# Projections inside the attention steps as two 64-row sums in two PSUM banks, one copied by ScalarE and the other added by VectorE

## The chip, the cores and the metric

The kernel runs on one core of a Trainium2 chip. The metric is the device time of that core in microseconds (us). A change of about 0.2% is the least that a measurement of this kernel can tell from no change.

The engines are named as in the profile: PE is TensorE's matmul, PEld its weight load, ACT is ScalarE, DVE is VectorE, POOL is GpSimd and SP is SyncE, which issues most DMAs here. PSUM is the memory that PE writes its sums to; it has eight banks of 128 partitions by 512 float32, and a bank must be read out by ACT or DVE before PE may start another sum in it.

## The reference

Two multi-head attentions over the same input are mixed by a gate. The sequence has S = 2048 rows, the model D = 640 features in 32 heads of 20.

```python
def attention(x, wqkv, wo):                      # once with A's weights, once with B's
    qkv = (x @ wqkv).reshape(B, S, 3, H, Dh).transpose(2, 0, 3, 1, 4)
    q, k, v = qkv[0], qkv[1], qkv[2]             # H = 32 heads, Dh = 20
    scores = einsum("bhqd,bhkd->bhqk", q, k) * Dh ** -0.5
    p = softmax(scores)
    o = einsum("bhqk,bhkd->bhqd", p, v)
    return o.transpose(0, 2, 1, 3).reshape(B, S, D) @ wo

x = A_x
g = sigmoid((x * gate_w).sum(-1, keepdims=True))
out = g * attention(x, A_wqkv, A_wo) + (1 - g) * attention(x, B_wqkv, B_wo)
```

## The kernel before

**Tiling.** The 64 heads of both attentions are worked off in 16 groups of four. A group has four blocks of 512 queries, and each block is eight steps, so there are 512 steps (`STEPS`). A step multiplies the keys of two 128-row tiles with the 512 queries of its block for four heads, which is eight sums of scores ("e" in the code, `scores`, lines L624 to L638), and takes the exponential of each with ACT out of PSUM (L635). The probabilities of the step before are multiplied with the values in two blocks "V" of four matmuls (`values`, L645 to L651), which collect in a bank of their own, `acc`. The largest score of each row, which the exponential subtracts, is found some 15 steps ahead by up to eight more sums of scores a step ("m", `max_mm`, L558 to L587). DVE reduces those (L585); for a part of them ACT takes a relu (L578) and DVE adds a second sum to it while it reduces (L582).

**Row groups.** A score needs only 60 or 64 rows of the array, because a head has 20 features (as high and low fp16 parts, and four rows more for the maximum). So sums of scores come in pairs: one in rows 0 to 63 and one in rows 64 to 127, at the same time and in two banks. A "V" and a projection use all 128 rows.

**Projections.** Inside the steps the next groups' queries, keys and values are projected, and the output projection of finished groups is made. Each is cut into slots "X": one sum of 9 to 15 matmuls over 128 rows (five tiles of 128 features, three products of high and low fp16 parts) in one bank, which one instruction reads. There are 456 such slots in the steps: 216 of `project_chunk` (L384 to L411, 176 or 168 columns, ACT copies at L402), 112 of the 128 of `project_v` (L519 to L535, 160 columns, ACT copies at L530), and 128 of `out_tiles` (L685 to L730; 64 of 160 columns that ACT copies at L715, 64 of 320 columns that DVE adds to the earlier output at L717). All their matmuls are issued by `mms` (L368 to L377, the matmul at L375). The first projections, ahead of the steps, go through the same lines with 512 columns.

**What sets the order.** The instructions are issued in an order that is written out by hand, and each engine works its own in that order. A string per step says where e, m, V and X stand:

```python
STEP = ("e0 m1 V e1 m0 e0 m1 e1 m0 e0 m1 e1 m0 V e0 m1 e1 m0",
        "X e0 m1 m0 e1 m0 m1 V m1 e0 e1 m0 e1 e0 V m0 e1 e0 m1",
        "X m0 m1 e0 m1 e0 e1 V e1 e0 m1 m0 V e1 m0 m1 m0 e0 e1 X")
```

The digit is the row group. The first string is for a step without a projection, the second for one slot, the third for two. Which string a step takes is set by how much is due (`behind`, L1044). The banks are given out by a clock that the program runs at build time: `take` (L122) picks among seven banks the one that comes free first by that clock, `give` (L133) says when a reader will be done with it, and `tick_score` and `tick_block` (L137 and L143) advance PE's time. `tick_block` adds `T_MODE` = 0.1 us on both sides of work on 128 rows. The clock only picks banks; the order of the work doesn't hang on it.

Of the kernel before, what the change touches and what calls it, by code (L numbers as in the profile page):

```python
# [61 lines left out]
def kernel(  # L62
# [18 lines left out]
    psum = ctx.enter_context(tc.tile_pool(name="psum", bufs=1, space=PSUM))  # L81
# [18 lines left out]
    acc = psum.tile([P, QB], F32, name="acc")  # L100
# [21 lines left out]
    def take():  # L122

        i = min((k for k in range(NB) if k not in held), key=lambda k: free_at[k])
        held.add(i)
        return i, banks[i]

# [32 lines left out]
    def scales(maxima, n, then):  # L160

        for _ in range(REST):
            yield
        yield PRODUCT
        i, pt = take()
        nc.tensor.transpose(pt[:n, :P], maxima[:, :n], ident)
        tick_block(0.1, free_at[i])
        yield
        e = wts.tile([5, 8], F32, name="e", tag="scl", bufs=2)
        nc.vector.tensor_reduce(e[:n, 0:1], pt[:n, :P], axis=AX.X, op=OP.max)  # L170
        give(i, spend("dve", 0.3, clock["done"]))
        spend("dve", 1.0)
        powers(e.bitcast(I32)[:n, :], 1)
        dg = wts.tile([5, 2, 5], F32, name="dg", tag="scd", bufs=2)
        for k in range(2):
            nc.vector.tensor_scalar(dg[:n, k, :n], ident[:n, :n], e[:n, 3 + k:4 + k], None, op0=OP.mult)
        for _ in range(REST):
            yield
        yield PRODUCT
        i, pb = take()  # L180
        tick_block(0.1, free_at[i])
        for k in range(2):
            nc.tensor.matmul(pb[:, k * n:(k + 1) * n], ones[:n, :], dg[:n, k, :n], start=True, stop=True)  # L183
        yield
        both = wts.tile([P, 10], F32, name="both", tag="scb", bufs=2)
        nc.vector.tensor_copy(both[:, :2 * n], pb[:, :2 * n])
        give(i, spend("dve", 0.2, clock["done"]))
        then(both[:, :n], both[:, n:2 * n])
# [179 lines left out]
    def mms(i, out_ap, pairs, cost):  # L368

        if now[0] >= 0:  # L370
            tick_block(len(pairs) * cost * T_SCORE, free_at[i])
        for k, (a, b) in enumerate(pairs):
            if now[0] < 0:
                tick_block(cost * T_SCORE, free_at[i])
            nc.tensor.matmul(out_ap, a, b, start=(k == 0), stop=(k == len(pairs) - 1))  # L375
            if now[0] < 0:
                yield  # L377
# [6 lines left out]
    def project_chunk(w, hi, lo, ch):  # L384

        wh, wl = w
        def pairs(n):
            if now[0] < 0:
                return ([(wh[:, c, :], b[:, c, n]) for c in range(NC) for b in (xh, xl)]
                        + [(wl[:, c, :], xh[:, c, n]) for c in range(NC)])  # L390
            return [(a[:, c, :], b[:, c, n]) for c in range(NC) for a, b in ((wh, xh), (wh, xl), (wl, xh))]

        t0 = ch * QB
        if now[0] >= 0:
            f = work.tile([P, QB], F32, name="fs")
            for k in range(3):
                if k:
                    yield
                m = slice(PARTS[k], PARTS[k + 1])
                i, pt = take()  # L400
                yield from mms(i, pt[:, m], pairs(slice(t0 + m.start, t0 + m.stop)), 0.34)
                nc.scalar.activation(f[:, m], pt[:, m], AF.Copy, scale=QKS)  # L402
# [116 lines left out]
    def project_v(gg, j):  # L519

        wh, wl = blk["v", gg]
        w = 161 if gg == 0 else 160
        for u in range(2):
            if u and now[0] >= 0:
                yield
            n = slice((j + u) * P, (j + u + 1) * P)
            i, pt = take()
            yield from mms(i, pt[:, :w], [(a[:, c, n], b[:, c, :w]) for c in range(NC) for a, b in
                                          ((xh, wh), (xh, wl), (xl, wh))], 0.33)
            nc.scalar.activation(V[gg % 2][:, j + u, :, 0:DH], pt[:, :160].rearrange("p (h d) -> p h d", h=2 * GH),  # L530
                                 AF.Copy, scale=QKS)
            give(i, spend("act", 0.25, clock["done"]))
            v_done.add((gg, j + u))
            if gg == 0:
                nc.scalar.activation(gates[:, 0, j + u:j + u + 1], pt[:, 160:161], AF.Exp, scale=inv_g)  # L535
# [16 lines left out]
    relus, relu_at = {}, {}  # L552
# [5 lines left out]
    def max_mm(u, ch, heads=(0, 1)):  # L558
# [9 lines left out]
        for j in heads:  # L568
            two = u < NS or ch < 2 and (j == 0 or g == 0)
            i, pt = take()  # L570
            ready = tick_score(j, i)
            r = slice(64 * j, 64 * j + 60)
            k = KD[g % 2 if ch == 0 else 1][r, pair] if two and ch % 2 == 0 else KT[g % 2][r, pair, ch * QB:(ch + 1) * QB]
            nc.tensor.matmul(pt, QT[g % 2][r, pair, q0:q0 + P], k, start=True, stop=True)  # L574
            m = mparts[g, qb][:, pair, j, t, ch:ch + 1]
            if two and ch % 2 == 0:
                relus[u, j] = start.tile([P, QB], F32, name="rl0", bufs=4) if u < NS else work.tile([P, QB], F32, name="rl", bufs=2)
                nc.scalar.activation(relus[u, j], pt, AF.Relu)  # L578
                back = relu_at[u, j] = spend("act", T_EXP, ready)
            elif two:  # L580
                rl = relus.pop((u, j))
                nc.vector.tensor_tensor_reduce(rl, pt, rl, 1.0, LOW, OP.add, OP.max, m)  # L582
                back = spend("dve", T_MAX, max(ready, relu_at.pop((u, j))))
            else:
                nc.vector.tensor_reduce(m, pt, axis=AX.X, op=OP.max)  # L585
                back = spend("dve", T_MAX, ready)
            give(i, back)  # L587
# [36 lines left out]
    def scores(G, kk, pair, heads=(0, 1)):  # L624
# [3 lines left out]
        for j in heads:  # L628
# [3 lines left out]
            nc.tensor.matmul(et, KT[g % 2][r, pair, kt * P:(kt + 1) * P],  # L632
                             QT[g % 2][r, pair, qb * QB:(qb + 1) * QB], start=True, stop=True)
            pt = pp.tile([P, QB], F32, name="pt")
            nc.scalar.activation(pt, et, AF.Exp, scale=factor(g // 4))  # L635
# [49 lines left out]
    def out_tiles(job, t, state):  # L685
# [17 lines left out]
        def products():  # L703
            wh, wl = wo_parts[z]
            for k in range(0, D, width):
                if k:
                    yield
                n = slice(k, k + width)
                i, pt = take()
                yield from mms(i, pt[:, :width], [(o[:p, a, c - c0], w[:p, c, n])  # L710
                                                  for c in range(c0, c1) for p in (P if c < full else 48,)
                                                  for a, w in ((0, wh), (0, wl), (1, wh))], width / QB)
                f = f_o[z][:, t:t + 1]
                if first:
                    nc.scalar.activation(y[:, n], pt[:, :width], AF.Copy, scale=f)  # L715
                else:
                    nc.vector.scalar_tensor_tensor(y[:, n], pt[:, :width], f, y[:, n], op0=OP.mult, op1=OP.add)  # L717
                give(i, spend("act" if first else "dve", 0.08 + width / 900, clock["done"]))
# [51 lines left out]
    def take_last():  # L770
# [5 lines left out]
        for t in range(4):  # L776
            nc.tensor.matmul(pt[:, 4 * t:4 * t + 4], ot[:, t * P:(t + 1) * P], one, start=True, stop=True)
        rc = work.tile([P, 16], F32, name="sq", bufs=2)
        nc.vector.reciprocal(rc, pt[:, :16])
        give(i, spend("dve", 0.3))  # L780
        i, pt = take()
        nc.tensor.transpose(pt[:16, :P], rc, ident)
        rt = wts.tile([16, P], F32, name="rt", tag="rt", bufs=1)
        nc.scalar.activation(rt, pt[:16, :P], AF.Copy)
        give(i, spend("act", 0.3))
        i, pt = take()
        for t in range(4):
            nc.tensor.matmul(pt[:, t * P:(t + 1) * P], picks[0].rearrange("p k e -> p (k e)")[:, t * P:(t + 1) * P], rt,
                             start=True, stop=True)
        o = work.tile([P, 2, QB], F16, name="on", bufs=2)  # L790
        for t in range(4):
            c = slice(t * P, (t + 1) * P)
            nc.vector.tensor_tensor(ot[:, c], ot[:, c], pt[:, c], op=OP.mult)
# [8 lines left out]
    def last_tiles(qb, o):  # L802
        wh, wl = wo_parts[2]
        for t in range(4):
            c = slice(t * P, (t + 1) * P)
            f = f_o[1][:, 4 * qb + t:4 * qb + t + 1]
            for half in range(2):
# [4 lines left out]
                for k, (a, w) in enumerate(((0, wh), (0, wl), (1, wh))):  # L812
                    nc.tensor.matmul(pt[:, :320], o[:, a, c], w[:, n], start=(k == 0), stop=(k == 2))  # L813
                if half and qb == NQ - 1 and t < 3:
                    part = pp.tile([P, QB], F32, name="pt")[:, :320]
                    nc.scalar.activation(part, pt[:, :320], AF.Copy, scale=f)
                    nc.gpsimd.tensor_tensor(y, y, part, op=OP.add)
                    give(i, spend("act", 0.42, clock["done"]))
                else:
                    nc.vector.scalar_tensor_tensor(y, pt[:, :320], f, y, op0=OP.mult, op1=OP.add)  # L820
# [35 lines left out]
    def turn(j0, c):  # L856
# [3 lines left out]
        for u in range(4):  # L860
            tick_block(0.11, free_at[i])
            nc.tensor.transpose(pt[:, u * P:(u + 1) * P], xs[:, j0 + u, c * P:(c + 1) * P], ident)  # L862
# [100 lines left out]
    start_stack.close()  # L963

# [212 lines left out]
```

## Time and profile before

| | |
|---|---|
| time, median of 3 runs | 2834.94 us (2834.72 to 2834.99) |
| span of the profiled execution | 2832.8 us, some 2.1 us less than the median |
| granted clock of TensorE | 0.996 |
| busy: PE, ACT, DVE, POOL | 98%, 89%, 86%, 24% |
| chain that ended last | PE 91%, DVE 5%, ACT 1% |

A profile row has the engine, the line in the code, the operation, its output and input tiles, their shape and the count; then the busy time in us, the mean of one in ns, and the idle time before with what ended it. A row of a timeline has the start in us, the duration in us, and then the same. Instructions of one kind that overlap or follow at once are merged into one row with their count. Durations of matmuls contain their way through the array, so that the distance between two starts tells the pace, not the duration.

### The profile page before, as it was taken

How to read it: one execution, taken by the hardware profiler on the slowest of the kernel's cores; microseconds unless marked ns; L12 is line 12 of the kernel's file. 1: busy time of each engine (PE TensorE's matmuls, PEld its weight loads, DVE VectorE, ACT ScalarE, POOL GpSimd, SP SyncE). 2: the span in 40 equal slices, each digit the busy share in tenths (PEclk: the TensorE clock that was granted, in tenths of full speed). 3: DMA queues.
4: the chain of work that ended last, by engine and by line, in shares of the span. 5: the costliest groups of instructions: out<-in, count | busy, mean ns of one | idle time of the engine just before them, and what ended most of it. 6: DMA issues, size and time to landing. Idle time of an engine off the chain costs nothing.

```text
span 2832.8 us, 62443 instructions
## 1 busy us (share of the span) xinstructions
PE 2773.1 (98%) x23362; PEld 970.8 (34%) x23362; DVE 2443.8 (86%) x4763; ACT 2529.7 (89%) x5122; POOL 671.8 (24%) x914
## 2 busy tenths in 40 slices
PE   6999999999999999999999999999999999999998
PEld 3533223342323323343233333334333333332222
DVE  6688999879999898988989888887888989989982
ACT  3799999989999999989999999998899999888887
POOL 5312113231221212233431111222112233120011
PEclk9999999999999999999999999999999999999999
DMA  4110101001020101202021020211202112122222
GB/s 135 35 45 7 39 6 42 16 16 29 13 52 16 37 11 27 47 13 50 17 56 44 14 60 16 48 37 24 49 15 61 38 38 70 55 71 60 63 60 74
DMA packets 167170, 113.71 MB, mean 40 GB/s; under 512 B 102224, under 2 KB 140808, under 8 KB 166864
## 3 DMA queue, kind: packets, MB, share of 16 engines
q1 hardware_dynamic: 164320, 108.09, 15.6%
q8 instruction: 183, 3.00, 0.4%
q0 software_dynamic: 1600, 0.96, 0.2%
q14 instruction: 123, 1.01, 0.1%
q10 hardware_dynamic: 944, 0.66, 0.1%
HBM read 48.89 MB, written 26.61 MB: 27 GB/s over the span
## 4 chain that ended last, share of the span: by engine, by line
PE 91%; DVE 5%; ACT 1%; DMA 1%; POOL 1%; issue 1%; SPq 0%; POOLq 0%; DVEq 0%; ACTq 0%
PE acc L650 34%; PE bank L375 20%; PE bank L632 19%; PE bank L574 17%; DVE mpart L585 3%; ACT pt L635 1%; DVE rl L582 1%; DMA xs<-in_A_x_dram 0%; ACT rl L578 0%; DMA wv<-in_A_wqkv_dram 0%; DVE ot L736 0%; PE bank L813 0%; PE bank L183 0%; PE bank L862 0%; DVE wmax L227 0%
## 5 line engine op out<-in xcount | busy, mean ns | idle before, releaser
L635 ACT ACTIVATE pt<-bank 128x512 f32<-128x512 f32 x4096 | 2157.5, 614 | 155.0 <-PE bank L632 75.1
L585 DVE TENSOR_REDUCE mpart<-bank 128x1 f32<-128x512 f32 x2976 | 1867.8, 681 | 264.3 <-PE bank L574 167.1
L650 PE MATMUL acc<-pt,v 128*21 128x512 f32 x8192 | 1082.0, 600 | 3.4 <-DVE ot L736 3.1
L632 PE MATMUL bank<-qt,kt 64*128 64x512 f16 x4096 | 1056.3, 380 | 11.9 <-ACT pt L635 4.5
L574 PE MATMUL bank<-kt,qt 60*128 60x512 f16 x3536 | 1013.0, 380 | 4.0 <-DVE mpart L585 0.7
L574 PEld LDWEIGHTS <-qt 60*128 60x128 f16 x4096 | 235.4, 94 | 686.6 <-issue 629.0
L632 PEld LDWEIGHTS <-kt 64*128 64x128 f16 x4096 | 248.1, 94 | 456.7 <-issue 322.8
L582 DVE CUSTOM_DVE_ANT_0 rl<-bank,rl 128x512 f32<-128x512 f32 x560 | 377.5, 678 | 20.5 <-ACT rl L578 8.2
L578 ACT ACTIVATE rl<-bank 128x512 f32<-128x512 f32 x560 | 329.8, 595 | 14.6 <-PE bank L574 12.3
L744 POOL TENSOR_TENSOR ot<-ot,sq 128x512 f32<-128x512 f32 x63 | 66.0, 1047 | 993.0 <-DVE sq L741 993.0
L650 PEld LDWEIGHTS acc<-pt,v 128*21 128x21 f32 x8192 | 143.0, 99 | 434.6 <-issue 421.5
L375 PE MATMUL bank<-xx,wbh 128*128 128x168 f16 (+2 forms) x2240 | 280.1, 244 | 3.2 <-ACT xx L866 1.9
L375 PE MATMUL bank<-xx,wbl 128*128 128x168 f16 (+2 forms) x1120 | 252.8, 243 | 0.0
L375 PEld LDWEIGHTS <-wbh 128*128 128x128 f16 x2240 | 183.6, 98 | 86.8 <-issue 79.8
L574 PE MATMUL bank<-kd,qt 60*128 60x512 f16 x560 | 203.6, 381 | 1.7 <-DMA kd<-dd 1.2
L375 PE MATMUL bank<-wvh,xx 128*128 128x160 f16 (+1 forms) x1280 | 155.4, 234 | 0.5 <-ACT pt L635 0.3
L375 PE MATMUL bank<-woh,o_in 128*128 128x160 f16 (+1 forms) x960 | 155.7, 256 | 0.0
L375 PEld LDWEIGHTS <-xx 128*128 128x128 f16 x1920 | 131.6, 97 | 52.7 <-issue 49.4
L404 POOL CAST cq<-fs 128x512 f16<-128x512 f32 x60 | 36.6, 609 | 446.0 <-ACT fs L402 444.0
L375 PE MATMUL bank<-wvl,xx 128*128 128x160 f16 (+1 forms) x640 | 137.3, 231 | 0.6 <-POOL wvl L315 0.6
L375 PEld LDWEIGHTS <-o_in 128*128 128x128 f16 (+1 forms) x1440 | 104.0, 97 | 75.3 <-issue 62.2
L402 ACT ACTIVATE fs<-bank 128x168 f32<-128x168 f32 (+1 forms) x216 | 67.5, 313 | 56.6 <-PE bank L375 40.0
(131 smaller groups left out, 1305.2 us busy)
## 6 DMA issues: line engine op xcount, KB each, us to landing
y_scr<-y_out SPq DMA_DIRECT2D x32, 320.0 KB
kt<-cq SPq DMA_DIRECT2D x120, 80.0 KB
o_scr<-on SPq DMA_DIRECT2D x240, 40.0 KB
kt<-cq SPq DMA_DIRECT2D x136, 40.0 KB
xs<-in_A_x_dram SPq DMA_DIRECT2D x8, 640.0 KB
o_in<-o_scr SPq DMA_DIRECT2D x32, 160.0 KB
y_out<-y_scr SPq DMA_DIRECT2D x16, 320.0 KB
xx<-y_scr SPq DMA_DIRECT2D x16, 320.0 KB
```

The costliest lines, as they stand in the source:

```text
L375: nc.tensor.matmul(out_ap, a, b, start=(k == 0), stop=(k == len(pairs) - 1))
L402: nc.scalar.activation(f[:, m], pt[:, m], AF.Copy, scale=QKS)
L404: nc.gpsimd.tensor_copy(hi, f)
L574: nc.tensor.matmul(pt, QT[g % 2][r, pair, q0:q0 + P], k, start=True, stop=True)
L578: nc.scalar.activation(relus[u, j], pt, AF.Relu)
L582: nc.vector.tensor_tensor_reduce(rl, pt, rl, 1.0, LOW, OP.add, OP.max, m)
L585: nc.vector.tensor_reduce(m, pt, axis=AX.X, op=OP.max)
L632: nc.tensor.matmul(et, KT[g % 2][r, pair, kt * P:(kt + 1) * P], QT[g % 2][r, pair, qb * QB:(qb + 1) * QB], start=True, stop=True)
L635: nc.scalar.activation(pt, et, AF.Exp, scale=factor(g // 4))
L650: nc.tensor.matmul(acc[32 * h:32 * h + VW, :], V[(g // 2) % 2][:, kt, (g % 2) * GH + h, :], ptiles.pop((G, kk, h)), start=(kt == 0), stop= ...
L744: nc.gpsimd.tensor_tensor(t3, t3, sq.unsqueeze(2).to_broadcast([P, 16, 32]), op=OP.mult)
```

## The change

In the steps, each slot's sum over 128 rows becomes two sums: one over rows 0 to 63, the other over rows 64 to 127, issued in turn (`halves_of`). Each goes to a bank of its own. The two banks must be neighbours, and `take_two` picks the pair whose later bank comes free first. Afterwards ACT copies the first bank to the target and DVE adds the second to it (`summed_halves`); where DVE added the sum before, it now adds both banks one after the other. The seven banks are one tile of seven parts in the steps, so that an instruction's access can lie in two of them, and the kernel itself states which readers don't depend on each other (`read`, `apart`). The number of columns, of slots and the strings are as before. A slot of 15 matmuls with 15 weight loads has now 30 of each.

```diff
+    def take_two():
+        i = min((k for k in range(NB - 1) if k not in held and k + 1 not in held),
+                key=lambda k: (max(max(free_at[k:k + 2]), clock["pe"]), abs(free_at[k] - free_at[k + 1])))
+        held.update((i, i + 1))
+        return (i, i + 1), store[0][:, i:i + 2]
...
+    def halves_of(pairs, w):
+        ik, two = take_two()
+        t = max(clock["pe"], max(rows_free), max(free_at[i] for i in ik))
+        parts = [[(a[p0:min(p0 + 64, a.shape[0])], b[p0:min(p0 + 64, a.shape[0])]) for a, b in pairs if a.shape[0] > p0]
+                 for p0 in (0, 64)]
+        for k in range(len(parts[0])):
+            for j in range(2):
+                if k < len(parts[j]):
+                    matmul(two[:, j, :w], *parts[j][k], start=(k == 0), stop=(k == len(parts[j]) - 1))
+        rows_free[:] = [t + len(parts[0]) * w / QB * T_SCORE] * 2
+        clock["pe"], clock["done"] = t, rows_free[0] + T_READY - T_SCORE
+        return ik, two[:, :, :w]
+
+    def summed_halves(ik, two, w, scale, to, shape=lambda x: x):
+        read(ik[:1], nc.scalar.activation(to, shape(two[:, 0]), AF.Copy, scale=scale))
+        give(ik[0], spend("act", 0.08 + w / 900, clock["done"]))
+        read(ik[1:], nc.vector.scalar_tensor_tensor(to, shape(two[:, 1]), scale, to, op0=OP.mult, op1=OP.add),
+             keep=[recent[-1][0]])
+        give(ik[1], spend("dve", 0.08 + w / 960, clock["act"]))
...
@@ project_chunk
-                m = slice(PARTS[k], PARTS[k + 1])
-                i, pt = take()
-                yield from mms(i, pt[:, m], pairs(slice(t0 + m.start, t0 + m.stop)), 0.34)
-                nc.scalar.activation(f[:, m], pt[:, m], AF.Copy, scale=QKS)
-                give(i, spend("act", 0.25, clock["done"]))
+                w = PARTS[k + 1] - PARTS[k]
+                ik, two = halves_of(pairs(slice(t0 + PARTS[k], t0 + PARTS[k + 1])), w)
+                summed_halves(ik, two, w, QKS, f[:, PARTS[k]:PARTS[k + 1]])
...
@@ out_tiles
                 if first:
-                    nc.scalar.activation(y[:, n], pt[:, :width], AF.Copy, scale=f)
+                    summed_halves(ik, two, width, f, y[:, n])
                 else:
-                    nc.vector.scalar_tensor_tensor(y[:, n], pt[:, :width], f, y[:, n], op0=OP.mult, op1=OP.add)
-                give(i, spend("act" if first else "dve", 0.08 + width / 900, clock["done"]))
+                    done = clock["done"]
+                    for j in range(2):
+                        read(ik[j:j + 1], nc.vector.scalar_tensor_tensor(y[:, n], two[:, j], f, y[:, n], op0=OP.mult,
+                                                                         op1=OP.add))
+                        give(ik[j], spend("dve", 0.08 + width / 960, done))
...
+    psum_start.close()
+    psum = ctx.enter_context(tc.tile_pool(name="psum_steps", bufs=1, space=PSUM))
+    store.append(psum.tile([P, NB, QB], F32, name="bank"))
+    banks[:] = [store[0][:, i] for i in range(NB)]
```

Four pieces of the order show what moves. In all of them a row is an instruction with its output and inputs, and in brackets stand the engines on whose semaphores it waits. `bank_89` to `bank_95` are the seven banks of before; `bank` is the one tile of after.

PE before, at the start of a slot of a value projection, behind a V; four sums of scores stand between the V and the slot:

```order
L650 MATMUL acc<-pt,v_86 21x512 x4
L574 LDWEIGHTS qt_80
L574 MATMUL bank_91<-kt_82,qt_80 128x512 [waits DVE_49]
L632 LDWEIGHTS kt_82
L632 MATMUL bank_95<-qt_80,kt_82 128x512 [waits Activation_49]
L632 LDWEIGHTS kt_82
L632 MATMUL bank_92<-qt_80,kt_82 128x512 [waits DVE_49]
L574 LDWEIGHTS qt_80
L574 MATMUL bank_93<-kt_82,qt_80 128x512 [waits Activation_49]
L375 LDWEIGHTS xx
L375 MATMUL bank_90<-wvh,xx 128x160 [waits Activation_49]
```

The slot takes one bank, `bank_90`, which none of the four sums ahead of it used.

PE after, at the start of the same slot, from the first sum behind the V:

```order
L157 LDWEIGHTS qt_83
L157 MATMUL bank<-kt_85,qt_83 128x512 [waits DVE_49]
L157 LDWEIGHTS kt_85
L157 MATMUL bank<-qt_83,kt_85 128x512 [waits Activation_49]
L157 LDWEIGHTS kt_85
L157 MATMUL bank<-qt_83,kt_85 128x512 [waits DVE_49]
L157 LDWEIGHTS qt_83
L157 MATMUL bank<-kt_85,qt_83 128x512 [waits Activation_49]
L157 LDWEIGHTS xx
L157 MATMUL bank<-wvh,xx 128x160 [waits Activation_49]
L157 LDWEIGHTS xx
L157 MATMUL bank<-wvh,xx 128x160 [waits DVE_49]
```

The slot now waits for two banks. Its first half takes the bank of the first `qt_83,kt_85` sum of this piece, the third ahead of the slot, so that it waits for that sum's exponential; its second half takes a bank that DVE read before the V.

PE after, behind the same slot:

```order
L157 MATMUL bank<-qt_83,kt_85 128x512
L157 LDWEIGHTS qt_83
L157 MATMUL bank<-kt_85,qt_83 128x512
L157 LDWEIGHTS qt_83
L157 MATMUL bank<-kd_87,qt_83 128x512 [waits DVE_49]
L157 LDWEIGHTS kt_85
L157 MATMUL bank<-qt_83,kt_85 128x512 [waits Activation_49]
L157 LDWEIGHTS qt_83
L157 MATMUL bank<-kt_85,qt_83 128x512 [waits DVE_49]
L157 LDWEIGHTS qt_83
L157 MATMUL bank<-kt_85,qt_83 128x512 [waits Activation_49]
L721 MATMUL acc<-pt,v_89 21x512 x4
```

With two banks in the slot, the first five sums take the five others, and the sixth, the last ahead of the V, waits for ACT's copy of the slot's first bank. Before, the slot's one bank was taken again only behind the V.

DVE after, between the two slots of that value projection:

```order
L656 TENSOR_REDUCE mpart<-bank 128x1 [waits PE_49] x2
L442 SCALAR_TENSOR_TENSOR v_89<-bank,v_89 128x8x20 [waits Activation_49]
L656 TENSOR_REDUCE mpart<-bank 128x1 [waits PE_49] x4
L651 ISA rl,mpart<-bank,rl 128x512 [waits PE_49]
L651 ISA mpart 128x1
L656 TENSOR_REDUCE mpart<-bank 128x1 [waits PE_49] x2
L442 SCALAR_TENSOR_TENSOR v_89<-bank,v_89 128x8x20 [waits Activation_49]
```

The additions at L442 are new on DVE; each waits for ACT's copy, and the reductions of the maximum stand behind it.

More of the change, by code (lines that the diff above doesn't have):

```diff
@@ L126, in take, with apart, on_bank, matmul @@
         return i, banks[i]
+    def take_two():
[3 more added lines that the diff above has]
+        return (i, i + 1), store[0][:, i:i + 2]
+    store, last_read = [], {}
+    fresh, recent = set(), []
+    def apart(ins, keep):
+        for r, engine in recent:
+            if r not in keep and engine != ins.engine:
+                tc.declare_no_dep(ins, r, reason="a reader of another bank")
+    def on_bank(out, ins, alone=True):
+        if store:
+            i = out.offset // QB
+            if alone:
+                apart(ins.ins, last_read.get(i, []))
+            fresh.add(i)
+        return ins
+    def matmul(out, a, b, start=True, stop=True, alone=True):
+        return on_bank(out, nc.tensor.matmul(out, a, b, start=start, stop=stop), alone)
+    def transpose(out, a, alone=True):
+        return on_bank(out, nc.tensor.transpose(out, a, ident), alone)
+    def read(banks_read, ins, keep=(), alone=True):
+        name = ins.ins.name
+        if store:
+            for i in banks_read:
+                if i in fresh:
+                    fresh.discard(i)
+                    last_read[i] = []
+                last_read[i].append(name)
+            if alone:
+                apart(ins.ins, keep)
+            recent.append((name, ins.ins.engine))
+            del recent[:-24]
+        return name
     def spend(engine, cost, ready=0.0):
@@ L526, in project_v @@
             n = slice((j + u) * P, (j + u + 1) * P)
[L527 to L532, printed above, removed]
+            pairs = [(a[:, c, n], b[:, c, :w]) for c in range(NC) for a, b in ((xh, wh), (xh, wl), (xl, wh))]
+            to = V[gg % 2][:, j + u, :, 0:DH]
+            if now[0] >= 0:
+                ik, two = halves_of(pairs, w)
+                summed_halves(ik, two, w, QKS, to, lambda x: x.rearrange("p (h d) -> p h d", h=2 * GH))
+            else:
+                i, pt = take()
+                yield from mms(i, pt[:, :w], pairs, 0.33)
+                nc.scalar.activation(to, pt[:, :160].rearrange("p (h d) -> p h d", h=2 * GH), AF.Copy, scale=QKS)
+                give(i, spend("act", 0.25, clock["done"]))
+                if gg == 0:
+                    nc.scalar.activation(gates[:, 0, j + u:j + u + 1], pt[:, 160:161], AF.Exp, scale=inv_g)
             v_done.add((gg, j + u))
[L534 to L535 removed]
     def sigmoids():
```

68 lines of the change are left out of this document (33 added, 35 removed).

## The prediction

> **What bounds the kernel now.** I read the page's busy times and its chain first, then the waits, then the timeline of single steps, and last the busy times of two stretches.
>
> ```profile
> span 2832.8 us, 62443 instructions
> PE 2773.1 (98%) x23362; PEld 970.8 (34%) x23362; DVE 2443.8 (86%) x4763; ACT 2529.7 (89%) x5122; POOL 671.8 (24%) x914
> PE 91%; DVE 5%; ACT 1%; DMA 1%; POOL 1%; issue 1%; SPq 0%; POOLq 0%; DVEq 0%; ACTq 0%
> PE bank L632 <- ACT pt L635: 4.5, 16, 0.5
> PE bank L632 <- DVE mpart L585: 2.7, 12, 0.2
> ACT pt L635 <- PE bank L632: 75.1, 275, 1.1
> DVE mpart L585 <- PE bank L574: 167.1, 300, 8.7
> ```
>
> PE is busy for 98% of the span and is 91% of the chain. The last four rows are waits (who waits, for whom, sum in us, count, longest): PE waits for a bank in only 28 places with 7.2 us together, while ACT and DVE wait for PE far longer. So PE sets the end, with seven banks in turn, and its waits for banks are nearly nothing. A step with one projection slot shows how PE's time goes:
>
> ```profile
> 1303.68 0.39 PE L574 MATMUL bank<-kt,qt 60*128 60x512 f16 x1
> 1303.69 0.60 PE L632 MATMUL bank<-qt,kt 64*128 64x512 f16 x2
> 1303.91 0.38 PE L574 MATMUL bank<-kt,qt 60*128 60x512 f16 x1
> 1304.22 0.32 PE L375 MATMUL bank<-xx,wbh 128*128 128x168 f16 x2
> ...
> 1305.25 0.24 PE L375 MATMUL bank<-xx,wbl 128*128 128x168 f16 x1
> 1305.42 0.39 PE L632 MATMUL bank<-qt,kt 64*128 64x512 f16 x1
> 1305.42 0.39 PE L574 MATMUL bank<-kt,qt 60*128 60x512 f16 x1
> 1305.64 0.38 PE L574 MATMUL bank<-kd,qt 60*128 60x512 f16 x1
> ```
>
> Pairs of sums (one in each row group) start 0.22 us apart: 1305.42 to 1305.64. The slot's 15 matmuls start from 1304.22 to 1305.25, so 0.0725 us apart (1.03/14, rounded by the ends). The last pair ahead of the slot started at 1303.91 and would have let the next pair start at 1304.13; the slot's first matmul starts at 1304.22, 0.09 later. Its last would have been through by 1305.32, and the next pair starts at 1305.42, 0.10 later. So a slot occupies PE for 1305.42 − 1304.13 = 1.29 us, of which 0.19 are the two changes between work on half the rows and work on all.
>
> ```profile
> 1303.68:1308.90 5.22, 5.22 (x51) 1.87 (x47) 4.38 (x9) 4.92 (x11) 1.76 (x2) 1.00 0.23 51
> 1002.70:1007.56 4.86, 4.50 (x36) 1.08 (x33) 4.72 (x11) 4.50 (x11) 0.83 (x3) 1.00 0.02 4
> ```
>
> These rows are the step with that slot and one without a slot (length; busy PE, PEld, DVE, ACT, POOL; the clock, 1.00). With a slot PE is busy throughout, ACT for 4.92 of 5.22 us and DVE for 4.38. Without one PE has gaps, and ACT and DVE set the pace.
>
> **The change, part by part.** Durations are of the profiled execution, whose span of 2832.8 us lies 2.1 us under the median of 2834.94; my sum is added to the median.
>
> *The two halves on PE.* The matmuls of a slot double from 15 to 30, but two go side by side, as pairs of scores do. The trace has no 64-row sum of 168 columns. From below: the pair takes as long as one matmul, 0.0725 us. From above: the halves, with a weight load each, go one after another, 0.145 us. Scores decide for the lower end: a pair with two loads and 512 columns needs 0.22 us, and 512 columns at the slot's pace are 0.0725 × 512/168 = 0.221. I add 0.004 us per pair for the second chain, since the fixed part of a matmul may not be shared: 15 × 0.0765 = 1.15 us.
>
> One rule on this stands in the Trainium skill, "TensorE: Matmul & The Clock Gate", section "LDWEIGHTS (loading the stationary operand)": a load's time goes by its columns, about columns/1.2 ns, and not by its rows; for 128 columns that is 107 ns, so a half would load as long as a whole, and two loads in series would be 213 ns a pair. By that the slot would be an estimated 3.2 us and the kernel some 870 us slower. The trace disagrees for loads that lie under matmuls, since load and matmul together need 0.0725 us there.
>
> *The changes of rows that go.* If a slot works on half rows there is no change of mode at either end: 0.19 us per run of slots. Of 456 slots in the steps, 48 steps carry two, one at each end, which lie next to a neighbour; I count 411 runs. The gain is 411 × 0.19 = 78 us, less 456 × 15 × 0.004 = 27: −51 us. ACT's 4.92 us of a 5.22 us step are the floor of it: 5.09 still lies above.
>
> *DVE's additions.* 216 + 112 + 64 = 392 new additions of 160 to 176 columns, and 64 more of 320.
>
> ```profile
> L717 DVE SCALAR_TENSOR_TENSOR xx<-bank,f_o,xx 128x320 f32<-128x320 f32 x32 | 17.4, 547 | 25.6 <-PE bank L632 20.3 <-PE bank L375 5.0
> L867 DVE SCALAR_TENSOR_TENSOR xx<-bank,both,xx 128x512 f16<-128x512 f32 x20 | 14.5, 748 | 5.2 <-ACT xx L866 5.1
> 1304.11 1.29 DVE L585 TENSOR_REDUCE mpart<-bank 128x1 f32<-128x512 f32 x2 [0.36 <-PE bank L632]
> L585 DVE TENSOR_REDUCE mpart<-bank 128x1 f32<-128x512 f32 x2976 | 1867.8, 681 | 264.3 <-PE bank L574 167.1
> ```
>
> From 320 to 512 columns the same kind grows by 201 ns, 1.05 ns a column, so 168 columns need 547 − 152 × 1.05 = 0.39 us. Two reductions of 681 ns take 1.29 us together, so some 0.07 of an instruction overlap with the next: 0.32 us. In sum 392 × 0.32 + 64 × 0.47 = 155 us on DVE. It is hidden where the slots are: there DVE goes from 4.38 to 4.70 of 5.09 us. The cover is DVE's idle 0.84 us in such a step; without it the 155 would stand on the path. Each addition waits for ACT's copy, and the reductions queue behind it; the copy starts right behind the slot (next fence), so this too falls into DVE's idle time. I take +10 us for steps where DVE is behind anyway, with bounds of 0 and 155.
>
> *The sixth sum behind the slot.* ACT's copies stay 392 in number and in width, but now one is waited for. In the order of after, the five sums behind a slot take the five free banks, and the sixth takes the bank that ACT copies. This is so in 311 of the 392 copied slots; in the others a V lies between.
>
> ```profile
> 1302.39 3.04 ACT L635 ACTIVATE pt<-bank 128x512 f32<-128x512 f32 x6 [0.20 <-PE bank L632]
> 1305.52 0.31 ACT L402 ACTIVATE fs<-bank 128x168 f32<-128x168 f32 x1
> 1305.84 0.60 ACT L635 ACTIVATE pt<-bank 128x512 f32<-128x512 f32 x1
> 1000.21 0.60 ACT L635 ACTIVATE pt<-bank 128x512 f32<-128x512 f32 x1 [0.33 <-PE bank L574]
> 1000.86 0.37 PE L632 MATMUL bank<-qt,kt 64*128 64x512 f16 x1 [0.25 <-ACT pt L635]
> ```
>
> The copy ends at 1305.83, 0.51 us behind the slot's stream (1305.32). The last two rows give the time from a reader's end to PE's start, 1000.81 to 1000.86: 0.05. So that bank is back at 0.56, and the sixth sum, in the third pair, is due at 0.44: +0.12 × 311 = +37 us. Slots that DVE alone reads are longer in DVE (0.55 twice); 41 of them have a sum that comes that early, up to 0.36 late, of which I take two thirds: +10 us.
>
> *Banks that are too young at the slot's start.* This is the largest term. A slot needs two neighbouring banks at once. Before, it took the bank free longest, seldom used by the last six sums. In the order of after, 145 of 455 slots take a pair of which one bank belongs to one of the last six sums, with neither a V nor a slot between: 1, 10, 35, 54, 36 and 9 of them for one to six sums back. A bank is held for at least 0.38 (the sum), 0.03 (1305.42 + 0.39 to 1305.84, the exponential's start), 0.61 (the exponential; page mean below) and 0.05 (release): 1.07, say 1.08 us. A sum k back started 0.11k earlier, so the slot, and PE in order behind it, waits 1.08 − 0.11k: 0.97 + 10 × 0.86 + 35 × 0.75 + 54 × 0.64 + 36 × 0.53 + 9 × 0.42 = 93 us.
>
> ```profile
> L635 ACT ACTIVATE pt<-bank 128x512 f32<-128x512 f32 x4096 | 2157.5, 614 | 155.0 <-PE bank L632 75.1
> L632 PE MATMUL bank<-qt,kt 64*128 64x512 f16 x4096 | 1056.3, 380 | 11.9 <-ACT pt L635 4.5
> ```
>
> From below this is 0, if the time comes back in steps that ACT bounds anyway; from above, a hold of 1.5 us, when the reader has another exponential ahead of it (0.506 us each, 3.04/6), gives 162 us. I stay at 93, because in a step with a slot PE has no gap in which to make up for it. What is late next is ACT: it runs dry while PE waits.
>
> *The rest.* One PSUM tile with its own statements on dependences moves no instruction; PE's order shows waits for the readers of the very bank alone. I cost it at nothing: no engine but PE would have to cover a wrong wait, and it would be a wait of PE for a bank. POOL's and SP's instructions and the DMAs stay as they are.
>
> Sum: −51 + 37 + 10 + 93 + 10 = +99 us; 2834.9 + 99 = 2934 us, 3.5% slower.
>
> **The rivals.**
>
> *A. The banks come back in time: faster.* The mechanism is the slack between banks and PE: if a pair of banks is back within 0.66 us on average (six sums at 0.11), neither the slot nor the sixth sum waits. For it speaks that PE hardly waits for a bank now (7.2 us); against it that the exponential alone holds a bank 0.61 us beyond the sum's 0.38. Then −51 + 10 remain: 2794 us. It decides from where the waits of 93 + 47 fall under 41 us.
>
> *B. The waits are absorbed in part.* A step without a slot is bound by ACT, and PE's lead there may pay for a wait at the next slot's start. With a quarter to half of the 140 us of waits: −51 + 10 + 35 to 70, 2829 to 2864 us. For it: PE's 4.50 of 4.86 us in such a step. Against it: slots come in most steps (378 of 512 by the strings).
>
> *C. The halves don't go side by side at this size.* The change then doesn't do what it says. With one load and matmul after another a slot is 15 × 0.145 = 2.18 us, against 1.29: +0.89 × 456 = +406, and fewer waits for banks: about 3240 us. For it: four PE instructions each 0.0725 us are more than any row here shows in a long stretch. Against it: pairs of scores.
>
> *D. DVE becomes the bound.* The 155 us come on top of the waits, since reductions hold their banks longer: some 3080 us. For it: 4.72 of 4.86 us DVE busy in a step without a slot. Against it: no slot stands there.
>
> **How the numbers follow.** The forecast has 0.62, B 0.18, A 0.10, C 0.06, D 0.04. The time is the forecast's, 2934. Its own range is 2865 (waits at half, DVE's at 10) to 3010 (a hold of 1.5 us gives 162 in place of 93). The range takes in B down to 2835 and leaves out A, C, D: 0.20. About 0.2%, 5.7 us, is the least that a measurement can tell from no change. Faster: A and a sixth of B, 0.13; same: 0.05, out of B; slower: the rest, 0.82.
>
> **What would show it.** Right: a pace of some 0.0765 us for pairs in a slot and no gap at its ends where the banks are old; PE's waits for banks rise from 7 to over 100 us, mostly ahead of a slot's first two matmuls and of the sixth sum behind it; ACT's and DVE's waits for PE grow; DVE's busy sum is some 150 us more; the busy share of PE falls under 95%. Wrong: a pace of pairs above 0.09 us (C), waits of PE under 40 us (A), DVE busy for over 95% of steps with a slot (D), or waits of DVE's additions for ACT that hold reductions back for longer than DVE's idle time.

## The result, and the profile after

The changed kernel takes 2983.55 us (2982.59 to 2986.14), the kernel before 2834.97: 1.0526 times as long, with a 95% interval from 1.0511 to 1.0541, or 149 us more. The forecast was 2934 us.

The page of the changed kernel, its chain and its waits (who waits for whom, sum in us, count, longest):

```profile
span 2984.1 us, 75456 instructions
PE 2826.7 (95%) x29626; PEld 1055.3 (35%) x29626; DVE 2574.5 (86%) x5219; ACT 2504.9 (84%) x5122; POOL 672.9 (23%) x914
PE 71%; DVE 14%; ACT 11%; issue 2%; DMA 1%; POOL 1%; SPq 0%; DVEq 0%; ACTq 0%; POOLq 0%
PE bank L157 <- ACT pt L706: 50.4, 162, 0.8
PE bank L157 <- DVE mpart L651: 24.2, 55, 1.1
PE bank L157 <- DVE mpart L656: 23.0, 57, 0.6
ACT pt L706 <- PE bank L157: 202.7, 503, 2.0
DVE fs L442 <- ACT fs L440: 137.1, 192, 9.3
```

PE was 91% of the chain and is now 71%; nearly all of the 20 points went to DVE (5% to 14%) and ACT (1% to 11%). These are the readers of banks that PE now waits for: 7 us of such waits before, 98 us in the three rows here. L157 is the one line from which the matmuls of sums and slots are now issued. Two slots in one place show both halves of the story:

```profile
1306.50 0.61 PE L721 MATMUL acc<-pt,v 128*21 128x512 f32 x4
1307.05 0.39 PE L157 MATMUL bank<-qt,kt 64*128 64x512 f16 x1
1307.05 0.60 PE L157 MATMUL bank<-kt,qt 60*128 60x512 f16 x3
1307.49 0.38 PE L157 MATMUL bank<-qt,kt 64*128 64x512 f16 x2
1308.36 0.32 PE L157 MATMUL bank<-xx,wbh 64*128 64x168 f16 x4 [0.49 <-DVE mpart L651]
...
1309.45 0.33 PE L157 MATMUL bank<-xx,wbh 64*128 64x176 f16 x4
...
1310.51 0.26 PE L157 MATMUL bank<-xx,wbl 64*128 64x176 f16 x2
1310.59 0.38 PE L157 MATMUL bank<-kd,qt 60*128 60x512 f16 x1
1310.60 0.38 PE L157 MATMUL bank<-kt,qt 60*128 60x512 f16 x1
```

The gain is there. The first slot's 15 pairs start at 1308.36 and the second slot's at 1309.45: 1.09 us or 0.0727 a pair (0.0725 within the rounding of the rows), and the pair of scores behind the second slot starts at 1310.59, one pair's time (0.075 for 176 columns) behind its last. No time is lost to a change of rows at either end. The loss stands ahead of the first slot. Its rows were free at 1307.49 + 0.22 = 1307.71, but it starts at 1308.36, since one of its two banks had been written by a sum of the burst at 1307.05 and was still being read by DVE:

```profile
1306.16 1.29 DVE L656 TENSOR_REDUCE mpart<-bank 128x1 f32<-128x512 f32 x2 [0.42 <-PE bank L157]
1307.61 0.69 DVE L651 CUSTOM_DVE_ANT_0 rl<-bank,rl 128x512 f32<-128x512 f32 x1 [0.16 <-PE bank L157]
1307.47 1.57 ACT L706 ACTIVATE pt<-bank 128x512 f32<-128x512 f32 x3 [0.36 <-PE bank L157]
```

DVE is done with that bank at 1308.30, and PE starts 0.06 later. The profile's 0.49 is the time in which PE did nothing at all; the slot is 0.65 late, because the last sums were still running for a part of it. Where only one half has to wait, less than half of it shows as idle:

```profile
1294.20 0.38 PE L157 MATMUL bank<-qt,kt 64*128 64x512 f16 x2
1294.42 0.23 PE L157 MATMUL bank<-xx,wbh 64*128 64x168 f16 x1
1294.82 0.30 PE L157 MATMUL bank<-xx,wbh 64*128 64x168 f16 x3 [0.18 <-ACT pt L706]
```

The first half starts its first matmul at 1294.42, and everything behind stands until 1294.82: 0.40 late, 0.18 of it idle. So I counted lateness instead, for every sum and slot in the steps: its start less the time at which its rows were free (the start of what ran there before, plus the columns of that at the pace of 0.0692 us for 160 and 0.0725 for 168). In the kernel before, the change of rows ahead of a slot (0.09 us in the timeline of the prediction) is not counted as lateness.

| late, in us, over the whole kernel | before | after |
|---|---|---|
| ahead of slots | 3.5 | 162 |
| of these, in slots with a bank from the last six sums, with neither V nor slot between | 1.5 (4 slots) | 109 (146 slots) |
| fourth to sixth sum behind a slot | 30 | 100 |

158 + 70 us more lateness, less the 78 us that the prediction counts for the two changes of rows, is 150 us; the spans differ by 151.3. That the two agree so closely is in part chance. The order of the program has 402 runs of slots, not 411, and 389 of them have a change ahead and 400 one behind, which makes some 75 us at 0.09 and 0.10. The twelfth sum behind a slot, the last ahead of the second V, is later by another 10 us than before and not in the table, and lateness of the two row groups at the same time is added up.

### The profile page after: what moved, and what is told of

Read it like the earlier page. It is cut to its first block, busy times and chain, and to the rows that moved or that the text cites. A ratio compares the mean times of both kernels' runs of the same rounds, so it can differ in the third digit from the quotient of the medians.

```text
span 2984.1 us, 75456 instructions
## 1 busy us (share of the span) xinstructions
PE 2826.7 (95%) x29626; PEld 1055.3 (35%) x29626; DVE 2574.5 (86%) x5219; ACT 2504.9 (84%) x5122; POOL 672.9 (23%) x914
## 3 DMA queue, kind: packets, MB, share of 16 engines
q14 instruction: 127, 1.04, 0.1%
## 4 chain that ended last, share of the span: by engine, by line
PE 71%; DVE 14%; ACT 11%; issue 2%; DMA 1%; POOL 1%; SPq 0%; DVEq 0%; ACTq 0%; POOLq 0%
PE bank L157 46%; PE acc L721 25%; ACT pt L706 10%; DVE mpart L656 9%; DVE rl L651 2%; ACT rl L647 1%; DVE ot L808 1%; DMA xs<-in_A_x_dram 0%; DVE ob L819 0%; DVE y_out L788 0%; DVE xx L788 0%; DMA wv<-in_A_wqkv_dram 0%; DVE wmax L276 0%; PE bank L160 0%; ACT fs L440 0%
## 5 line engine op out<-in xcount | busy, mean ns | idle before, releaser
L157 PE MATMUL bank<-qt,kt 64*128 64x512 f16 x4096 | 1089.4, 379 | 14.3 <-ACT pt L706 4.2
L157 PE MATMUL bank<-kt,qt 60*128 60x512 f16 x3536 | 1060.6, 378 | 7.5 <-DVE mpart L656 1.1
L157 PEld LDWEIGHTS <-qt 60*128 60x128 f16 x4096 | 260.7, 94 | 688.9 <-issue 656.5
L157 PEld LDWEIGHTS <-kt 64*128 64x128 f16 x4096 | 269.0, 94 | 416.1 <-issue 326.7
L157 PE MATMUL bank<-xx,wbh 64*128 64x168 f16 (+2 forms) x4400 | 294.5, 238 | 45.6 <-ACT pt L706 16.0
L157 PEld LDWEIGHTS <-wbh 64*128 64x128 f16 (+1 forms) x4400 | 230.8, 94 | 116.1 <-issue 86.9
L157 PE MATMUL bank<-xx,wbl 64*128 64x168 f16 (+2 forms) x2200 | 258.2, 237 | 0.0
L157 PE MATMUL bank<-kd,qt 60*128 60x512 f16 x560 | 202.8, 380 | 1.9 <-DMA kd<-dd 1.2
L157 PE MATMUL bank<-wvh,xx 64*128 64x160 f16 (+1 forms) x2400 | 165.4, 230 | 27.6 <-ACT pt L706 14.7
L442 DVE SCALAR_TENSOR_TENSOR fs<-bank,fs 128x168 f32<-128x168 f32 (+1 forms) x216 | 72.3, 335 | 138.2 <-ACT fs L440 137.1
L157 PE MATMUL bank<-woh,o_in 64*128 64x160 f16 (+2 forms) x1856 | 159.5, 250 | 23.9 <-ACT pt L706 14.6
L157 PEld LDWEIGHTS <-xx 64*128 64x128 f16 (+1 forms) x3600 | 146.4, 94 | 72.1 <-issue 55.5
L157 PEld LDWEIGHTS <-o_in 64*128 64x128 f16 (+1 forms) x2784 | 123.9, 94 | 81.0 <-issue 56.4
```

Of the source, the lines that this page charges most:

```text
L157: return on_bank(out, nc.tensor.matmul(out, a, b, start=start, stop=stop), alone)
L442: read(ik[1:], nc.vector.scalar_tensor_tensor(to, shape(two[:, 1]), scale, to, op0=OP.mult, op1=OP.add), keep=[recent[-1][0]])
```

## The experiments

The theory: the halves gain what they should, and the banks take it back, because two of seven are wanted at once, and neighbours at that. Rival 1: VectorE's additions cost it. Rival 2: the one PSUM tile with its stated dependences makes false waits. Times are medians, with the ratio to the kernel before on the same chip and its 95% interval.

### Any two banks

```diff
     def take_two():
-        i = min((k for k in range(NB - 1) if k not in held and k + 1 not in held),
-                key=lambda k: (max(max(free_at[k:k + 2]), clock["pe"]), abs(free_at[k] - free_at[k + 1])))
-        held.update((i, i + 1))
-        return (i, i + 1), store[0][:, i:i + 2]
+        ik = tuple(sorted((k for k in range(NB) if k not in held), key=lambda k: free_at[k])[:2])
+        held.update(ik)
+        return ik, [banks[i] for i in ik]
```

> The slots keep their two halves, ScalarE's copy and VectorE's addition, but the two banks need not be neighbours: each slot takes the two banks that come free first. Theory (waits for banks that are too young, because neighbours are wanted): the 162 us that PE lost ahead of the slots in the changed kernel fall to 30 to 70 us, the sixth sum behind the slot still waits (some 50 us), so 2850 to 2890 us. Rival 1 (VectorE's additions are what costs): they stay, so over 2950 us. Rival 2 (the one PSUM tile and its stated dependences make false waits): they stay, 2984 us.

2893.12 us, 1.0207 (1.019 to 1.0224): 90 us of the 149 come from the demand for neighbours alone. Page and waits of this kernel:

```profile
PE 2806.2 (97%) x29626; PEld 1058.4 (37%) x29626; DVE 2569.2 (89%) x5219; ACT 2496.9 (86%) x5122; POOL 671.7 (23%) x914
PE bank L156 <- ACT pt L705: 20.6, 105, 0.5
PE bank L156 <- DVE mpart L655: 6.8, 26, 0.5
```

The lateness ahead of slots falls from 162 to 52 us, as expected; the additions are all still there. Rival 2's 2984 and rival 1's 2950 are both ruled out as the main cause. But 2893 lies just above the range, and the fourth to sixth sum behind a slot are now 123 us late, not 100: a part of the wait that went ahead of the slot comes back behind it.

### Whole slots in the one tile

In short, at each of the projections:

```diff
-    ik, two = halves_of(pairs, w)
-    summed_halves(ik, two, w, scale, to)
+    i, pt = take()
+    for k, (a, b) in enumerate(pairs):
+        matmul(pt[:, :w], a, b, start=(k == 0), stop=(k == len(pairs) - 1))
+    read([i], nc.scalar.activation(to, shape(pt), AF.Copy, scale=scale))
```

> The slots are whole again (one sum over 128 rows in one bank, one reader), but the seven banks are one tile with the stated dependences, as in the changed kernel. Theory: 2835 us, within 6 us. Rival 2 (false waits from the one tile): more than 2850 us, up to 2984 us if it were all of the loss. Rival 1 says nothing here but 2835 us, since there are no additions.

2834.57 us, 1.0004 (0.9994 to 1.0013). The tile and its statements cost nothing with whole slots. With halves, the run with any two banks has the same tile and the same statements and is 90 us faster, so rival 2 is out as the main cause.

### The additions alone, and the changed kernel nearly without them

Whole slots with an addition of 0 times the same bank behind the copy:

```diff
     read([i], nc.scalar.activation(to, shape(pt), AF.Copy, scale=scale))
+    read([i], nc.vector.scalar_tensor_tensor(to, shape(pt), 0.0, to, op0=OP.mult, op1=OP.add), keep=[recent[-1][0]])
```

> The slots are whole, as in the run with one tile, and behind ScalarE's copy VectorE adds the same bank times 0 to the target: the additions alone, 392 of them, with their wait for the copy, but one bank only. Theory (the additions are hidden in VectorE's idle time): VectorE's busy sum rises by some 130 us, the time by 0 to 25 us, 2835 to 2860 us. Rival 1 (the additions cost): 2930 to 2985 us.

2866.03 us, 1.0114 (1.0097 to 1.013), 32 us more; DVE's busy time rises from 2444.0 us (whole slots in the one tile) to 2530.7. A little over the theory's range, far under rival 1's. The other way round, the changed kernel with an addition of one column, which leaves the rest of the second half's sum out of the result:

```diff
-    read(ik[1:], nc.vector.scalar_tensor_tensor(to, shape(two[:, 1]), scale, to, op0=OP.mult, op1=OP.add),
+    a = shape(two[:, 1])
+    one = (slice(None),) + (slice(0, 1),) * (len(a.shape) - 1)
+    read(ik[1:], nc.vector.scalar_tensor_tensor(to[one], a[one], scale, to[one], op0=OP.mult, op1=OP.add),
```

> The changed kernel, neighbours and all, but the addition takes one column alone, so that the second half's sum is left out of the result but for that column. Theory: VectorE's busy sum falls by some 60 to 110 us, and as its second bank comes back earlier only by some 0.2 us behind the slot, the time falls by 0 to 25 us: 2955 to 2984 us. Rival 1: the time falls by most of what VectorE gains, to under 2910 us.

2973.64 us, 1.0493 (1.0476 to 1.0511): 10 us less. The same cut in the kernel with any two banks:

> Any two banks, but the addition takes one column alone, so that the second half is left out of the result but for that column. Theory: the additions cost in this kernel about what they cost alone (32 us), less the wait for the copy that stays: 2865 to 2885 us. If the additions make up the most of what is left (58 us over the kernel before and the 78 us of gain), under 2850 us; if they are hidden, 2890 us.

2884.56 us, 1.0173 (1.0156 to 1.019): 9 us less than with any two banks, where I had expected 8 to 28. So the width of the additions is worth some 10 us in both kernels. Most of these 10 us show at one place: the twelfth sum behind a slot, 10 us later than before in the changed kernel, is only 3 us later with the narrow addition. That the additions cost 32 us alone points to what a narrow addition keeps, the wait for the copy and a bank that comes back later, though no run shows the two apart. In the run with the additions alone the sixth sum behind a slot is 34 us late in place of 18, the twelfth is 7 us later than before and the fifth 3 us, together 26 of the 32; the rest was not traced. Rival 1 is out as the main cause: the additions' share is 10 us by their width, and 32 with all that they bring in whole slots. No run has the halves without any addition.

### A second bank kept out of use

```diff
     i, pt = take()
+    held_too[i] = take()[0]
...
     give(i, spend("act", 0.25, clock["done"]))
+    give(held_too[i], free_at[i])
```

> The slots are whole, in one bank with one reader, but a second bank (the next that comes free) is kept out of use from the slot's start until its reader is given back; nothing is written to it. So only the bank that is missing behind a slot is tried, without halves, additions or a wait for a second bank at the slot's start. Theory (a missing bank makes the fourth to sixth sum behind a slot wait): 30 to 80 us more, 2865 to 2915 us, with waits of PE at these sums. Rival 3 (one bank less behind the slot is no matter, and what is left over in the run with any two banks is the waits at the slot's start and the additions): 2835 to 2845 us.

2849.51 us, 1.0052 (1.0035 to 1.0068): 15 us, between the theory's 30 and the 10 at most of rival 3. The fourth to sixth sum behind a slot are late by 53 us here (30 before). One bank less behind a slot costs something, but by itself little: whole slots also leave 0.1 us more, the change of rows, before these sums are due.

### Five sums on either side of the slot

In the string for one slot, the slot goes one sum later (with halves in any two banks, the rows that are free first beginning), and the same string in the kernel before, as control:

```diff
-        "X e0 m1 m0 e1 m0 m1 V m1 e0 e1 m0 e1 e0 V m0 e1 e0 m1",
+        "e0 X m1 m0 e1 m0 m1 V m1 e0 e1 m0 e1 e0 V m0 e1 e0 m1",
```

> Halves in any two banks, and in steps with one slot the slot stands one sum later, so that five sums stand between the V and the slot and five between the slot and the next V (four and six before); the row group that is free first begins its half first. Theory: the sixth sum behind the slot no longer waits (it stands behind a V), so the 75 us there fall to under 25 us; the waits at the slots' start stay at some 50 us: 2820 to 2870 us. If the time stays at 2880 to 2900 us, the wait of the sixth sum was not on the path.

> The kernel before with the slot one sum later, as in the run with five and five, as its control. A lone sum ahead of a slot over all rows leaves the other row group idle for some 0.1 us, and one behind it too: 330 x 0.1 to 0.2 us, 2865 to 2900 us; if pairs form otherwise, 2835 us.

2948.15 us, 1.04 (1.0383 to 1.0418), and the control 2897.07 us, 1.0221 (1.0204 to 1.0238). My expectation for the halves failed. The move costs 55 us with halves and 62 us without. For whole slots 30 to 65 us were expected, because an odd number of sums leaves one row group idle. I had left that out of the expectation for the halves, but it need not be their reason: there the free row group begins first, and the order of the two halves' matmuls goes by the program's clock. Counted as before, the lateness ahead of the slots rose from 52 to some 105 us in that run. What makes up its 55 us is not shown. The lateness of the fifth and sixth sum behind the slot together only went from 97 to 81 us: it moved to the fifth, which is 5 us late in the control. So it is not ScalarE's copy of the slot's bank alone that these sums wait for; the other banks are short too.

### Halves one after the other, each beside sums of scores

Built from the kernel before: the first half runs in rows 0 to 63 while five sums of scores run in rows 64 to 127, then a V, then the second half with the rows exchanged. A slot holds one bank at a time.

```diff
-        "X e0 m1 m0 e1 m0 m1 V m1 e0 e1 m0 e1 e0 V m0 e1 e0 m1",
+        "X e1 m1 e1 m1 e1 V e0 m0 e0 m0 e0 V m1 e0 e1 m0 m1 m0",
...
+        for h in range(2):
+            part = [(a[64 * h:min(64 * h + 64, a.shape[0])], b[64 * h:min(64 * h + 64, a.shape[0])])
+                    for a, b in pairs if a.shape[0] > 64 * h]
+            i, pt = take()
...
+            for k, (a, b) in enumerate(part):
+                while k and n < 5 and rows_free[1 - h] <= t + 0.02:
+                    emits[0](tokens.pop(0))
...
+                nc.tensor.matmul(pt[:, :w], a, b, start=(k == 0), stop=(k == len(part) - 1))
...
+            give(i, (second if h else first)(pt[:, :w]))
```

> Built from the kernel before. In steps with one slot the two halves stand one after the other, each beside five sums of scores in the other row group, with a V between them; ScalarE copies the first half, VectorE adds the second. So a slot holds one bank at a time, for the length of a half, and no work on all rows is left but the V; the sums around it come at half the pace, so that a bank's last reader has twice the time. Theory (the halves' gain is real and the banks ate it): waits of PE for banks stay near those of before, the gain of some 78 us stands against some 32 us for the additions: 2775 to 2830 us. If a half beside sums doesn't go at the pace of the pairs, or the order feeds ScalarE worse, over 2835 us.

2989.12 us, 1.0547 (1.0529 to 1.0565): a miss by 160 us. The timeline of PE shows a second half that runs as planned, and the burst of six sums behind it ahead of the next slot:

```profile
1022.16 0.24 PE L402 MATMUL bank<-wvh,xx 64*128 64x160 f16 x1
1022.17 0.39 PE L678 MATMUL bank<-qt,kt 64*128 64x512 f16 x1
...
1022.39 0.38 PE L620 MATMUL bank<-kd,qt 60*128 60x512 f16 x1
...
1022.61 0.38 PE L678 MATMUL bank<-qt,kt 64*128 64x512 f16 x1
...
1024.35 0.39 PE L620 MATMUL bank<-kt,qt 60*128 60x512 f16 x1
1024.35 0.60 PE L678 MATMUL bank<-qt,kt 64*128 64x512 f16 x2
1024.57 0.59 PE L620 MATMUL bank<-kt,qt 60*128 60x512 f16 x3
1025.01 0.23 PE L402 MATMUL bank<-wvh,xx 64*128 64x160 f16 x1
1025.45 0.37 PE L678 MATMUL bank<-qt,kt 64*128 64x512 f16 x1 [0.21 <-ACT pt L681]
```

Beside the half the sums keep their 0.22 us (1022.17, 1022.39, 1022.61), so the half costs PE's other rows nothing. But six sums and the slot's bank are seven banks; the next sum, due with the half at 1025.01, waits until 1025.45 for a bank of the first pair of the six, the one that ACT reads. Over the kernel the first sum behind a slot's start is 138 us late. It is the same cause in a new place, which I had made with the string. To test that, the burst was spread: two sums behind the first half, two behind the second, two ahead of the next slot.

```diff
-        "X e1 m1 e1 m1 e1 V e0 m0 e0 m0 e0 V m1 e0 e1 m0 m1 m0",
+        "X e1 m1 e1 m1 e1 m0 m1 V e0 m0 e0 m0 e0 e1 m0 V m1 e0",
```

> As the run with the halves beside sums, but the six sums that stood in one burst ahead of a slot are spread: two behind the first half, two behind the second half and two ahead of the next slot, so that no burst of six stands together with a slot's bank. Theory (that run lost its gain to sums that waited for the banks of a burst of six): some 0.4 us less in each of some 330 steps, 2840 to 2890 us, and under 2835 us if all banks come back in time. If the time stays near 2989 us, the loss there was not the banks but the order itself (ScalarE or VectorE fed worse).

2874.67 us, 1.014 (1.0123 to 1.0157): 114 us less by the place of six sums, within the range. The first sum behind a slot's start is now 6 us late over the whole kernel. What is left stands at the seventh, 97 us late. This is the quickest of the kernels with halves, and none of them beats the kernel before.

## Why the prediction was right, and where its terms were off

- **PE is the bound, and waits for banks become the loss.** Right: the chain and the waits above. The kernel is 149 us slower; 99 were forecast, and the 2983.55 us lie in the range up to 3010.
- **The pace of pairs.** Forecast 0.0765 us with 0.004 for the second chain; measured 0.0727 for 168 columns. The two chains share all of the pace, the 27 us taken off the gain were wrong, and the gain is some 75 us (402 runs of slots in place of 411), not 51. Rival C is out with it. By the rule of the Trainium skill ("TensorE: Matmul & The Clock Gate", section "LDWEIGHTS (loading the stationary operand)") a load's time goes by its columns, which gives an estimated 107 ns for 128 columns. That does not set the pace here: two such loads and two matmuls pass in 73 ns. The profile's rows have 98 ns for a load of 128 rows before and 94 ns for one of 64 rows after, so the number of rows hardly matters to a load, as the page says.
- **No change of rows.** Right: none at 1309.45 and 1310.59.
- **Young banks at the slot's start.** The mechanism was right: 145 slots and 93 us were forecast, 146 slots and 109 us measured, and lifting the demand for neighbours gave 90 us back. What it left out are the other 310 or so slots, costed at nothing, with 53 us. The hold of 1.08 us was that of a bank that ACT reads at once; in the example above DVE was the reader, and the bank came back 1.31 us after the start of its sum, 0.65 us after the rows were free. The prediction's upper bound of 162 us is a slip: by its own sum a hold of 1.5 us gives 154, and the top of the range would be 2995 us in place of 3010, which the result is also under. That the lateness measured ahead of all slots is 162 us too is chance.
- **The sixth sum behind the slot.** Forecast 37 + 10 us; measured 70 us for the fourth to sixth sum, of which the sixth has 54 (72 against 18 before) and the two ahead of it 16. The bank of the copy is one cause; the runs with five sums and with a bank kept out of use show that the others are short too.
- **The additions.** One takes 0.335 us in the trace (0.39 forecast), all of them 131 us of DVE's busy time (155 forecast). Their width is worth 10 us, as the sum had it; alone they cost 32.

```profile
L442 DVE SCALAR_TENSOR_TENSOR fs<-bank,fs 128x168 f32<-128x168 f32 (+1 forms) x216 | 72.3, 335 | 138.2 <-ACT fs L440 137.1
```

- **The one tile.** Costed at nothing, and so measured.
- **The sum.** The step that was mis-sized is the lateness: 163 us from 109 + 53 at the slots' start, where 93 stood, and 70 behind them, where 47 stood. A gain that was some 24 us larger than forecast hid a part of that. So the time lies in the range partly by luck: two terms were too small and the gain too small as well.
- **The rivals.** A and B (banks back in time, or waits absorbed in part) fell: PE lost more, not less. Rival D fell: DVE's share stayed at 86%.
- **What would show it.** PE's waits for banks were to rise over 100 us; the three rows have 98, and the lateness 232, since the view counts only time in which no matmul is running in either row group. PE's busy share fell from 98 to 95%, about as forecast. ACT's waits for PE grew (75 to 203 us ahead of the exponentials), but DVE's did not: the idle time before its reductions fell from 264 to 67 us, and DVE waits for ACT's copies ahead of the additions (137, 55 and 36 us) instead. That sign the prediction had wrong.

Open are the last 6 of the 32 us of the additions alone, the 55 us of the slot moved by one sum with halves, and which reader holds the banks that the 310 other slots wait for in each case.

## What to carry to other kernels

Before two sums go side by side to save time on PE, count the banks: how long each is held (here 1.08 us by the prediction's rows, 1.31 in the example), how many sums are issued in that time, and what the slot would take from them. A rule that makes neighbours of two buffers picks by place and not by age; it cost 90 of 149 us here, which a free choice of two gave back. The place of a burst in the order can weigh as much as the number of buffers: six sums moved gave 114 us.

## What the runs showed of the hardware that was not expected

Two 64-row sums of 168 columns, each matmul with its own weight load, run at 0.0727 us a pair, within rounding the pace of one 128-row sum (0.0725), and a 64-row half beside sums of 512 columns leaves these at 0.22 us. The change between work on half and on all rows costs some 0.09 and 0.10 us, and none of it is left between half-row work of different kinds (1309.45 and 1310.59). In one example a wait for a bank that concerned one row group showed in the waits with less than half of what it cost (0.18 of 0.40 us).
